# Three more late attention units in 128-byte runs: q and k in 32 or 64 loads a unit instead of 8 or 16, scores in one insertion instead of two

## The chip, the cores and the metric

The kernel runs on one core of a Trainium2 chip. The metric is the device time of one execution in microseconds (us). Engines are named as in the profile: PE (TensorE, the matmuls), PEld (its weight loads), DVE (VectorE), ACT (ScalarE), POOL (GpSimd) and SP (SyncE, which here only issues DMAs). Every engine takes its instructions in the order in which the program has them.

## The reference

Attention within chunks of 64 tokens, and two MLPs behind it, all in float32. q, k and v are (batch 8, heads 8, seq 576, head_dim 64); the 4608 tokens are 18 units of 256.

```python
def _attn_ref(q, k, v):
    ...
    scores = scale * np.matmul(q_c, k_c.transpose(0, 1, 2, 4, 3))
    scores = scores - np.max(scores, axis=-1, keepdims=True)
    attn = np.exp(scores)
    attn = attn / (np.sum(attn, axis=-1, keepdims=True) + 1e-09)
    out = np.matmul(attn, v_c)
    ...
def _moe_ref(x, w_gate, w_val, w_out, rms_g):      # 512 -> 1536 -> 512
    rms = np.sqrt(np.mean(x * x, axis=-1, keepdims=True) + 1e-06)
    xn = x / rms * rms_g
    g = xn @ w_gate
    silu = g * (1.0 / (1.0 + np.exp(-g)))
    val = xn @ w_val
    return (silu * val @ w_out).astype(np.float32)

def _moe2_ref(x, w_in, w_out):                     # 512 -> 2048 -> 512
    h = x @ w_in
    relu6 = np.clip(h + 3.0, 0.0, 6.0)
    g = h * relu6 / 6.0
    return (g @ w_out).astype(np.float32)
```

## The kernel before

The big matmuls run on pairs of numbers that are split into a high and a low part, and with sums and differences of blocks in place of some products (as in Strassen's scheme), so that most of the weights come from scratch tensors in device memory. The program goes in ticks. On a tick PE gets a group of big products, and an agenda says which other steps are put into the program at that tick. Tokens go through the first MLP in passes; in the second and third of these (366 to 765 us) the attention of later tokens is computed between the products: units 10 to 13 in the first, 14 to 17 in the second, at 0, 14, 28 and 42 ticks from its start, of 66. A pass has first the products with operands `xu` and `wo` (L1016; each `wo` load of 512 KB serves 12 of them and is issued at L463 six loads ahead of its use), then those with `gs` and `wd` (L1030, L1031, L1033; `wd` loads at L469, 512 KB).

A unit has these steps, each at a tick of its own after the unit's start (`STEPS_P`): q and k are transposed in blocks of 32 on DVE (`turn_q` at 0, `turn_k` at 1), scores on PE and their row maxima on DVE (3 and 5), the subtraction (6), exp (7), the sum and its inverse (9), the transposes of p on PE (11), the product with v (13) and squares for the RMS norm (14). Buffers for q, k, qT, kT, p and v exist once: q of the next unit can be loaded only when `turn_q` of this one is over, k when `turn_k` is.

There are two classes. `Wide`, the class of units 11, 12, 13, 15, 16 and 17, loads q and k in runs of 8 tokens of a head (2 KB in device memory), so that a 32 x 32 block transpose leaves 32 of the 64 head dimensions on a partition group; a score is the sum of two products on 32 rows, and the heads are done in two halves, `scores0`/`top0` and `scores1`/`top1`. `Pair`, the class of units 10 and 14 (and of those before 10), loads runs of 32 numbers (128 bytes), so that all 64 head dimensions stand on partitions after the transpose; one `scores` does all heads on 64 rows, one `top` all maxima. `WHOLE` names the units from 10 on that are `Pair`, and `plan_unit` then leaves out the second scores and maxima:

```python
                    if i in WHOLE and st in ("scores0", "top0"):
                        st = st[:-1]
                    elif i in WHOLE and st in ("scores1", "top1"):
                        continue
```

A unit whose 256 tokens lie in one sequence is one run of the function `runs`; where it crosses the end of a sequence of 576 it is two. Unit 13 (tokens 3328 to 3583, sequence end at 3456) is two runs of 128 tokens, units 12 and 17 are one. `Wide` issues 4 loads for each of q and k and each run (L886), `Pair` 16 (L746 or L750):

```python
                            for a in range(NP):
                                nc.sync.dma_start(out=d[r:r + 32, a, u0:u0 + un, :], in_=sv[j, g, :, a])
```

All loads go out on SP's queue. Attention loads are handed out from a list, 3 on each tick (`some(3)`), behind the wo or wd loads of that tick. `turn_k` of a unit puts the next unit's q and k into the list, `values` the next unit's v; before `turn_q` all loads of that unit which are still in the list are issued at once (`until(("qk", i))`). Every DMA of SP and of ACT takes one of eight semaphores (DMAHW0 to DMAHW7) in rotation, and an engine that issues a DMA waits until the one that had this semaphore last has landed. ACT issues the stores into scratch tensors (L286, L290: `stash_in`, `stash_out`).

Of the kernel before, what the change touches and what calls it, by code (L numbers as in the profile page):

```python
# [54 lines left out]
""".split()  # L55
SHARE_V, LOW_V = (), (2, 3)

WHOLE = (10, 14)

STEPS_P = (  # L60
    (0, ("turn_q",)),
# [30 lines left out]
def fused_kernel(  # L92
# [1004 lines left out]
    with tc.manual_schedule():  # L1097
# [24 lines left out]

        unit = [(Pair if i < 10 or i in WHOLE else Wide)(i) for i in range(NPR)]
        chain = [Half(i) for i in range(NTL, 2 * NTL)] + unit[4:]
# [37 lines left out]
        def plan_unit(i, t0):  # L1162
            for d, steps in STEPS_H if i < NTL else STEPS if t0 < P0 else STEPS_P:
                for st in steps:
# [4 lines that stand above are left out]
# [689 lines left out]
```

## Time and profile before

| | |
|---|---|
| median of 3 runs | 1649.12 us (1648.95 to 1649.36) |
| profiled execution | 1649.82 us |
| its span | 1648.0 us |
| granted TensorE clock, mean | 1.000 |
| busy: PE, DVE, ACT, POOL | 99%, 63%, 51%, 28% |
| DMA moved | 375 MB, mean 228 GB/s |

The span goes from the first to the last instruction of one profiled execution. A share is busy time over the span; engines work beside each other, so shares say which engine has time left, and only a wait on PE itself says what an edit elsewhere costs. "DMA share" in a window is the mean busy share of the 16 DMA engines.

### The profile page before, as it was taken

The page shows a single profiled execution, that of the slowest core. Times are in us where ns is not written, and L with a number is a line of the kernel's source. Part 1 is how long each engine was busy: PE and PEld are TensorE (multiplying, and loading weights), DVE is VectorE, ACT ScalarE, POOL GpSimd, SP SyncE. Part 2 cuts the span into 40 slices and gives each one's busy share as a digit, 9 for nine tenths or more (in the row PEclk, how much of TensorE's full clock was granted, in tenths as well). Part 3 has the DMA queues.
Part 4 walks back from the last instruction along what each step waited for, and adds up shares of the span by engine and source line. Part 5 has one row for each costly group of instructions (what it writes and reads, how often), then busy time and mean ns, then how long its engine had stood idle before and what let it go on. Part 6 is the DMA issues. An engine that isn't in the chain of part 4 may idle for free.

```text
span 1648.0 us, 26265 instructions
## 1 busy us (share of the span) xinstructions
PE 1636.9 (99%) x9807; PEld 1348.0 (82%) x9807; DVE 1034.8 (63%) x1532; ACT 846.0 (51%) x1410; POOL 453.4 (28%) x331
## 2 busy tenths in 40 slices
PE   8999999999999999999999999999999999999998
PEld 7888887888888888788888888888888888888887
DVE  7997566655575755638334388358746764874475
ACT  6885445455454555645434344455545544654553
POOL 1002434322236423354226522140024003301310
PEclk9999999999999999999999999999999999999999
DMA  9914777748988698855979685667877796788666
GB/s 294 287 46 108 206 211 208 209 157 243 313 277 231 203 295 269 282 216 209 331 238 334 258 283 198 219 194 244 216 216 228 213 239 200 219 230 230 191 202 156
DMA packets 352223, 375.06 MB, mean 228 GB/s; under 512 B 201440, under 2 KB 277216, under 8 KB 351968
## 3 DMA queue, kind: packets, MB, share of 16 engines
q1 hardware_dynamic: 282208, 302.32, 60.2%
q10 hardware_dynamic: 69888, 71.06, 12.7%
q8 instruction: 78, 1.28, 0.3%
q14 instruction: 49, 0.40, 0.1%
HBM read 292.55 MB, written 80.74 MB: 227 GB/s over the span
## 4 chain that ended last, share of the span: by engine, by line
PE 93%; DVE 2%; DMA 2%; SPq 2%; issue 1%; ACT 1%; POOL 0%; ACTq 0%; DVEq 0%; POOLq 0%
PE PS L1016 37%; PE PS L1595 18%; PE PS L1005 13%; PE PS L1030 6%; PE PS L1031 6%; PE PS L1033 6%; SPq L750 1%; PE PS L1042 1%; PE PS L1039 1%; PE PS L1038 1%; PE PS L837 1%; DMA q<-in_q_dram 1%; PE PS L1796 1%; PE PS L819 1%; PE PS L910 1%
## 5 line engine op out<-in xcount | busy, mean ns | idle before, releaser
L1016 PE MATMUL PS<-xu,wo 128*128 128x512 f32 x1512 | 349.8, 391 | 0.7 <-DVE s L1370 0.7
L1016 PEld LDWEIGHTS PS<-xu,wo 128*128 128x128 f32 x1512 | 282.3, 188 | 60.3 <-DVE s L1370 1.1
L1016 PE MATMUL PS<-xo,wq 128*128 128x512 f32 x1344 | 305.3, 389 | 0.0
L1595 PE MATMUL PS<-gs,wq 128*128 128x512 f32 x1296 | 295.3, 389 | 0.0
L1016 PEld LDWEIGHTS PS<-xo,wq 128*128 128x128 f32 x1344 | 252.3, 188 | 52.4
L1595 PEld LDWEIGHTS PS<-gs,wq 128*128 128x128 f32 x1296 | 242.9, 188 | 51.8 <-DVE gs L1589 1.2
L1005 PE MATMUL PS<-XH,w 128*128 128x512 f32 x576 | 146.2, 395 | 1.0 <-DVE w L222 1.0
L1005 PEld LDWEIGHTS PS<-XH,w 128*128 128x128 f32 x576 | 106.2, 188 | 24.6 <-DVE w L222 1.8
L1030 PE MATMUL PS<-gs,wd 128*128 128x512 f32 x288 | 113.2, 393 | 0.0
L1031 PE MATMUL PS<-gs,wd 128*128 128x512 f32 x288 | 112.2, 390 | 0.0
L1061 POOL TENSOR_TENSOR al<-sg,ah 128x512 fp32r<-128x512 f32 x40 | 55.9, 1396 | 155.7 <-ACT ah L1059 149.9
L1366 POOL TENSOR_TENSOR gs<-gu,gs 128x512 fp32r<-128x512 f32 x60 | 84.5, 1427 | 46.2 <-ACT gs L1365 36.3
L1370 DVE TENSOR_TENSOR gu<-gu,PS 128x512 f32<-128x512 f32 x60 | 41.1, 686 | 84.4 <-ACT gu L1452 44.1
L1663 POOL TENSOR_TENSOR gt<-gx 128x512 f32<-128x512 f32 x8 | 10.4, 1294 | 296.5 <-DVE gx L1660 296.5
L1589 DVE TENSOR_TENSOR gs<-gu,gs 128x512 fp32r<-128x512 f32 x88 | 68.0, 792 | 31.9 <-ACT gs L1588 31.6
L1588 ACT CAST gs<-gt 128x512 fp32r<-128x512 f32 x96 | 58.2, 623 | 44.1 <-DVE gt L1732 30.7
L1525 DVE SCALAR_TENSOR_TENSOR gu<-gu,PS 128x512 f32<-128x512 f32 x48 | 32.8, 684 | 72.9 <-ACT gu L1522 72.9
L1005 PE MATMUL PS<-XL,w 128*128 128x512 f32 x288 | 77.2, 390 | 0.0
L1033 PE MATMUL PS<-gs,wd 128*128 128x512 f32 x288 | 77.0, 389 | 0.0
L1059 ACT CAST ah<-sg 128x512 fp32r<-128x512 f32 x52 | 32.4, 624 | 75.5 <-DVE sg L1350 41.3
L1588 ACT CAST gs<-gu 128x512 fp32r<-128x512 f32 x96 | 57.3, 620 | 25.0 <-DVE gs L1589 17.7
L1663 POOL TENSOR_TENSOR gt<-gu 128x512 f32<-128x512 f32 x24 | 32.6, 1359 | 129.0 <-DVE gu L1660 124.8
(254 smaller groups left out, 2828.0 us busy)
## 6 DMA issues: line engine op xcount, KB each, us to landing
wq<-stash_in SPq DMA_DIRECT2D x128, 512.0 KB
wo<-ops SPq DMA_DIRECT2D x126, 512.0 KB
wq<-sums_out SPq DMA_DIRECT2D x64, 512.0 KB
wq<-stash_out SPq DMA_DIRECT2D x48, 512.0 KB
wd<-keep_out SPq DMA_DIRECT2D x36, 512.0 KB
yd<-yst SPq DMA_DIRECT2D x18, 512.0 KB
ops<-w ACTq DMA_DIRECT2D x36, 256.0 KB
v<-in_v_dram SPq DMA_DIRECT2D x32, 256.0 KB
```

Source lines behind the costliest of these rows:

```text
L1005: nc.tensor.matmul(ps, w(wi, c), xs[c][xi], start=(i == 0), stop=(i == n - 1))
L1016: nc.tensor.matmul(PS[:, bank, :], op[:, wi, c * 128:(c + 1) * 128], x[xi][:, c, :], start=first and i == 0, stop=last and i == 5, skip_gr ...
L1030: nc.tensor.matmul(ps, wm[0], a[0], start=first, stop=False)
L1031: nc.tensor.matmul(ps, wm[1], a[0], start=False, stop=False)
L1033: nc.tensor.matmul(PS[:, banks[m], :], w[:, 0, m * 128:(m + 1) * 128], a[1], start=False, stop=last)
L1061: nc.gpsimd.tensor_tensor(lo, t, hi.bitcast(F32), op=ALU.subtract)
L1366: e.tensor_tensor(w[:, 1, :], t, w[:, 0, :].bitcast(F32), op=ALU.subtract)
L1370: nc.vector.tensor_tensor(o, x, y, op=op)
L1588: nc.scalar.copy(w[:, 0, :], x)
L1589: e.tensor_tensor(w[:, 1, :], x, w[:, 0, :].bitcast(F32), op=ALU.subtract)
L1595: nc.tensor.matmul(PS[:, banks[m], :], op[:, wi, m * 128:(m + 1) * 128], x[xi], start=first and (wi, xi) == (0, 0), stop=False, skip_group ...
L1663: nc.gpsimd.tensor_tensor(slot(i, "t"), slot(i, "12"), slot(i, "11"), op=ALU.subtract)
```

## The change

`WHOLE` gains units 12, 13 and 17. They go from class `Wide` to class `Pair`.

```diff
-WHOLE = (10, 14)
+WHOLE = (10, 12, 13, 14, 17)
```

On PE, in the part with `xu` and `wo`, unit 12's scores stand like this (rows of the difference, - before, + after; L945 belongs to an RMS norm, L819 transposes unit 12's p):

```order
 L945 MATMUL PS<-sqh,ones_r 128x512
 L1016 MATMUL PS<-xu,wo 128x512 x12
-L910 MATMUL PS<-kT,qT 64x64 x32
-L1016 MATMUL PS<-xu,wo 128x512 x24
-L910 MATMUL PS<-kT,qT 64x64 x32
-L1016 MATMUL PS<-xu,wo 128x512 x72
+L781 MATMUL PS<-kT,qT 64x64 x32
+L1016 MATMUL PS<-xu,wo 128x512 x96
 L819 MATMUL PS<-ident,p 128x128 x8
```

The second insertion is gone, and the first stands where it stood. Units 13 and 17 change in the same way, among the products with `wd`.

On SP the loads of unit 13 stand, before, between the last `wo` and the first `wd` loads of the pass (numbers at scratch tensors as the program has them; v is unit 13's):

```order
L886 DMA k<-in_k_dram 16x2x512 x4
L463 DMA wo<-ops_124 128x1024 x2
L469 DMA wd<-keep_out_125 128x1024
L469 DMA wd<-keep_out_126 128x1024
...
L758 DMA v<-in_v_dram 128x8x64 x2
L469 DMA wd<-keep_out_131 128x1024
L469 DMA wd<-keep_out_132 128x1024
```

and after the change, from the first `wd` load of the pass on:

```order
L469 DMA wd<-keep_out_125 128x1024
L469 DMA wd<-keep_out_126 128x1024
L750 DMA q<-in_q_dram 32x4x32 x6
L469 DMA wd<-keep_out_127 128x1024
...
L469 DMA wd<-keep_out_130 128x1024
L750 DMA k<-in_k_dram 32x4x32 x3
L469 DMA wd<-keep_out_131 128x1024
L750 DMA k<-in_k_dram 32x4x32 x25
L758 DMA v<-in_v_dram 128x8x64 x2
L469 DMA wd<-keep_out_132 128x1024
```

The last four k loads stood two loads ahead of the first `wd`; now the last 25 stand behind the seventh. From the first q of unit 13 to its last k there are 78 loads on SP, 64 of q and k, 7 `wo` and 7 `wd`; before there were 21, 16 and 5 `wo`. In all SP issues 96 more DMAs.

With the semaphores that each waits for, the first k loads of unit 13 stand like this in the new order of SP:

```order
L469 DMA wd<-keep_out_127 128x1024 [waits DMAHW2_49,PE_49]
L469 DMA wd<-keep_out_128 128x1024 [waits DMAHW3_49]
L750 DMA q<-in_q_dram 32x4x32 [waits DMAHW5_49]
L750 DMA q<-in_q_dram 32x4x32 [waits DMAHW6_49]
L750 DMA k<-in_k_dram 32x4x32 [waits DMAHW7_49,DVE_49]
L750 DMA k<-in_k_dram 32x4x32 [waits DMAHW0_49]
```

and on ACT, whose DMAs take part in the same rotation, at that place:

```order
L1361 ACTIVATE gu<-PS 128x512 [waits PE_49]
L1452 COPY gu<-PS 128x512 [waits PE_49]
L286 DMA stash_in_113<-sc 128x2x256 [waits DMAHW4_49,Activation_49]
L286 DMA stash_in_113<-slo 128x2x256 [waits DMAHW7_49,Pool_49]
L1361 ACTIVATE gu<-gu 128x512 [waits DVE_49]
```

The DMAHW7 that the first k waits for was last taken by the second of these two stores; 34 more loads follow on SP up to unit 13's last k.

## Rows read from the trace of the kernel before

**Rows 1.** the page: busy time and share of each engine; the chain that ended last.
```profile
PE 1636.9 (99%) x9807; PEld 1348.0 (82%) x9807; DVE 1034.8 (63%) x1532; ACT 846.0 (51%) x1410; POOL 453.4 (28%) x331
...
PE 93%; DVE 2%; DMA 2%; SPq 2%; issue 1%; ACT 1%; POOL 0%; ACTq 0%; DVEq 0%; POOLq 0%
```

**Rows 2.** timeline of PE around unit 12's scores: start, length, engine, line, operation, tiles, count.
```profile
420.29 5.73 PE L1016 MATMUL PS<-xu,wo 128*128 128x512 f32 x24
425.95 1.16 PE L910 MATMUL PS<-kT,qT 32*64 32x64 f32 x64
427.04 16.62 PE L1016 MATMUL PS<-xu,wo 128*128 128x512 f32 x72
443.49 0.71 PE L819 MATMUL PS<-ident,p 128*128 128x128 f32 x5
```

**Rows 3.** timeline of PE at unit 14's scores.
```profile
576.28 1.16 PE L781 MATMUL PS<-kT,qT 64*64 64x64 f32 x64
577.37 5.97 PE L1016 MATMUL PS<-xu,wo 128*128 128x512 f32 x25
```

**Rows 4.** timeline of DVE: the q turns of units 12, 14 and 17.
```profile
458.22 2.27 DVE L890 STREAM_TRANSPOSE qT<-q 128x1024 f32<-128x1024 f32 x1
...
569.64 1.24 DVE L762 STREAM_TRANSPOSE qT<-q 128x1024 f32<-128x1024 f32 x1
...
699.14 2.16 DVE L890 STREAM_TRANSPOSE qT<-q 128x1024 f32<-128x1024 f32 x1
```

**Rows 5.** windows: stretch, its length, PE, PEld, DVE, ACT, POOL busy, PEclk, DMA share, GB/s.
```profile
124.00:139.00 15.00, 14.80 (x93) 11.64 (x92) 11.09 (x21) 8.84 (x14) 0.00 (x0) 1.00 0.21 33
...
485.00:500.00 15.00, 15.00 (x130) 12.37 (x129) 9.42 (x14) 10.12 (x17) 8.52 (x7) 1.00 1.01 363
...
501.90:524.00 22.10, 22.10 (x215) 18.03 (x214) 10.65 (x15) 9.45 (x15) 12.77 (x10) 1.00 0.95 255
...
525.00:530.00 5.00, 5.00 (x24) 4.09 (x23) 1.23 (x2) 0.56 (x2) 3.31 (x3) 1.00 0.01 0
```

**Rows 6.** timeline of SP's queue: loads of units 12, 13 and 17.
```profile
415.71 1.28 SPq L886 DMA_DIRECT2D q<-in_q_dram  x3
...
460.51 1.28 SPq L886 DMA_DIRECT2D q<-in_q_dram  x3
...
477.07 1.83 SPq L886 DMA_DIRECT2D k<-in_k_dram  x4
...
494.66 1.29 SPq L758 DMA_DIRECT2D v<-in_v_dram  x2
...
659.39 1.33 SPq L886 DMA_DIRECT2D q<-in_q_dram  x3
```

**Rows 7.** timeline of PE at unit 13's first scores.
```profile
505.63 1.16 PE L910 MATMUL PS<-kT,qT 32*64 32x64 f32 x64
```

**Rows 8.** timeline of SP's queue: loads of unit 4 (first two) and unit 14.
```profile
110.53 12.43 SPq L750 DMA_DIRECT2D q<-in_q_dram  x24
123.06 16.32 SPq L750 DMA_DIRECT2D k<-in_k_dram  x32
...
501.94 1.42 SPq L750 DMA_DIRECT2D q<-in_q_dram  x3
...
514.59 9.35 SPq L750 DMA_DIRECT2D k<-in_k_dram  x14
```

**Rows 9.** waits of SP's queue, 459 to 497: who waited <- for what: sum, times, longest.
```profile
SPq L463 <- DMA stash_in<-slo: 4.7, 1, 4.7
...
SPq L758 <- DMA stash_in<-slo: 0.5, 1, 0.5
```

**Rows 10.** timeline of ACT's DMA issues: two stores of a stash.
```profile
470.95 0.56 ACTq L286 DMA_DIRECT2D stash_in<-slo  x1
...
484.99 0.43 ACTq L286 DMA_DIRECT2D stash_in<-slo  x1
```

**Rows 11.** issues by line: L750: count, ns min/median/max, first and last start.
```profile
L750 SPq DMA_DIRECT2D q<-in_q_dram x144: 311/448/1505, 90.9 to 513.9; - x144
```

## Prediction

> **What bounds the kernel now.** I read the busy table first. TensorE works for 99% of the span and the next engine, VectorE, for 63%; the chain of waits says the same, 93% of its length is PE [rows 1]. Two things follow. Work that PE no longer does comes off the time at its full length, and a wait that PE has to take goes on top at its full length, since PE has no slack anywhere later in which to make it up. VectorE, ScalarE and the DMA queues matter here only where PE stands waiting for them. So I then read the PE timeline at the places where the late units put their scores among the big products, and the timelines of VectorE and of SP's queue around them, to see by how much each unit's q and k come ahead of their use.
>
> **What the change takes off PE.** Before, a Wide unit puts its scores into the row of big products twice, 32 instructions each time, of which the trace holds two records each (x64). In unit 12 both insertions are to be seen [rows 2]: 24 big products between them take 420.29 to 425.95, and the insertion itself holds PE from 425.95 to 427.04, 1.09 us. What it costs is a little more, for the products beside it lose some overlap. The stretch from 427.04 to 443.49 holds 72 products, 0.2285 us each; 24 of them would be 5.48 us, and from 420.29 to the end of the second insertion at 427.04 there are 6.75 us. One insertion so costs 6.75 - 5.48 = 1.27 us. The one that stays (L781, whole heads on 64 rows) holds PE from 576.28 to 577.37 in unit 14, 1.09 us as well [rows 3]: twice the rows cost no more, and the second insertion goes without anything in its place. Three units, one insertion less in each: 3 x 1.27 = 3.8; with a little for the wider gaps that I see beside the other insertions I take **-3.9 us**.
>
> **What it takes off VectorE** is worth nothing. Both turns of a unit fall from 2.2 us (L890) to 1.24 us (L762) each [rows 4], and two maxima become one. VectorE is 63% busy and PE waits for none of this, with one exception, below.
>
> **What it adds to SP's queue.** A unit's q and k come in 32 DMAs instead of 8, and unit 13, which lies across the end of a sequence, takes 64 of 16 KB instead of 16 of 64 KB. That is 24 + 48 + 24 = 96 more issues, all on SP, which issues in order, between the weight loads (wo, wd) for the products. Packets also shrink: with 128-byte runs alone the queue moved 33 GB/s at a share of 0.21, 157 GB/s at a full share; with long runs 363 at 1.01, 359 GB/s [rows 5]. A unit's q and k are 1.05 MB, so they take 6.7 us of all the DMA engines against 2.9, about 4 more per unit.
>
> Units 12 and 17 have room. Unit 12's loads began at 415.71 and its q is turned at 458.22; 43 issues stand there in the new order (32 and 11 wo), and at 0.65 us each (below) they end at 443.7. Unit 17's begin at 659.39 and end at 687.4 by the same price, while its q is turned at about 699 [rows 4, 6]. The wo and wd among them go out later by some us. They are loaded six ahead, and six times 12 products of 0.2285 us are 16 us, more than the 24 further issues cost (24 x 0.65 = 15.6), if hardly. I cost both units at nothing; if that cover is not whole, 0 to 2 us each.
>
> Unit 13 has no room. Its q cannot be loaded before unit 12's q has been turned out of the single buffer: 458.22, with the shorter turn over at 459.5 [rows 4]. Before, its 16 loads and the 5 wo among them went out from 460.51 to 478.90, and what followed was two wo, then wd and v [rows 6]. In the new order 78 issues stand from the first q to the last k, 64 small ones, 7 wo and 7 wd, and the last 25 are k alone. When is the last k there? PE reaches unit 13's scores at 505.63 before [rows 7], 1.3 earlier once unit 12 has saved its insertion: 504.3. The k turn of 1.24 us has to come first, so k must have landed by 503.1. (The order puts turn_q before it, which has its data by then.)
>
> The price of an issue is what decides. The trace has the same form of load in two settings. In unit 14, among wd loads and at a DMA share of 0.95 [rows 5], 34 issues go from 501.94 to 523.94, 0.65 us each; in unit 4, the very shape of unit 13's (64 of 16 KB, few other DMAs, share 0.21), 56 issues go from 110.53 to 139.38, 0.515 us each [rows 8]. The difference is waiting: a DMA may go only when the one 8 back in a common rotation of SP's and ACT's has landed. Unit 13's loads fall into the stretch where the share is 1.01 at its end [rows 5], and stand behind wo and wd of 512 KB, so it is nearer to unit 14. I take 0.65: 459.5 + 78 x 0.65 = 510.2. The last one lands some 2.5 us after that (an estimate: the last k of unit 14 in that stretch is issued at 523.5 and the share from 525 on is 0.01 [rows 5, 8]): 512.7. That is 512.7 - 503.1 = **9.6 us too late**.
>
> A second working, from one wait, says the same. In the new order the first k of unit 13 waits for the rotation's DMAHW7, which the second of ACT's stores of a stash holds; ACT issued it at 484.99, as its compute gets there, which follows PE. A store of this kind took about 5.7 us at the place before (issued 470.95; SP's wo waited 4.7 us for it, until just before 477.07), and this very one about 10.6 (SP's second v waited 0.5 us for it and went out at 495.57) [rows 6, 9, 10]. Now 128-byte DMAs stand ahead of it in place of wd, so I take 5.7, and its issue 1.3 earlier with all of PE's work: 483.7 + 5.7 = 489.4. The 35 issues from there at 0.65 end at 512.1, at 0.515 at 507.4; with the landing 514.6 and 509.9, so 11.5 or 6.8 us late. I stay with 9.6, between them.
>
> The bounds: if the store lands in 2.5 us (486.2) and each issue takes 0.475 (the median L750 row of 0.45 with its gap [rows 11]), the last k lands at 486.2 + 16.6 + 2.5 = 505.3, 2.2 us late. If nothing waits for the store at all and unit 4's pace holds, it lands at 459.5 + 78 x 0.515 + 2.5 = 502.2, in time. Upwards, the store takes 10.6 us (494.3) and each issue 0.65: 519.5, 16.4 us late.
>
> What is late next: PE stands at L781 with all the wd products of the down phase behind it in order, so it waits and nothing overtakes it. VectorE stands at turn_k, with the clean-up of the weight halves behind it; they are made well ahead. Unit 14's q waits for turn_q of unit 13 and its loads stand behind the late k; they move by some us, and unit 14's scores are only at 576.28, 70 us on [rows 3]. So the stall is paid once.
>
> **The sum.** 1648.0 (span) - 3.9 + 9.6 = 1653.7; the profiled execution took 1649.82 in all, so 1655.5; it lies 0.7 above the median of the runs, 1649.12, and against that median I predict **1654.8 us**.
>
> **Rivals.**
> *In time (faster).* SP's pace is the one of unit 4. Then the loads are there at 502.2 and only the gain is left: 1645.2. For it: an issue itself takes 0.45 [rows 11]; the deciding point is (503.1 - 2.5 - 459.5) / 78 = 0.53 us per issue, just above unit 4's 0.515. Against it: the DMA engines have no idle time there, the share is 1.01 from 485 on, and the wait for ACT's store is not in that pace. 0.15.
> *Half late (no change that can be told).* A stall of 0.6 to 7.2 us eats the gain. The mean of the second working at 0.515 (6.8) and of its lower bound (2.2) is 4.5, so 1649.12 - 3.9 + 4.5 = 1649.7. For it: the 25 last k issues stand together with no wd among them, and unit 4's pace is theirs. 0.27.
> *Late in full,* a stall of 7.2 to 16.4 us: my forecast, 1652.4 to 1661.6. 0.55.
> *A load costs by its count.* If a DMA of 16 KB took as long as one of 64 KB did, the 64 loads would take four times the 18.4 us that the 16 took (460.51 to 478.90 [rows 6]), 73.6 us: 533.1, with 2.5 and 1.24 a stall of 32.5 us, 1677.7. Against it: unit 4's 16 KB go at 0.515. 0.03. This would be the rule of the Trainium skill, "DMA: Bandwidth & Descriptors", "Rules for kernel authors": "Many small transfers | Coalesce into one large transfer; under 64 KB you're paying mostly overhead". The trace agrees that the packets are dearer, not that the price goes by the count alone.
>
> A difference of under 0.2%, 3.3 us, is about what these measurements cannot tell from none. So: slower 0.55 + 0.03 = 0.58 (a stall over 7.2), no difference 0.27, faster 0.15. **Range**: from 1646.0, within the case of no stall, to 1661.5, near the upper bound of the stall; it leaves out about 0.1 at either end. The likeliest case alone is 1652.4 to 1661.5.
>
> **What would show it.** In the new profile PE should stand idle once for 5 to 16 us just ahead of unit 13's L781, near 504, and the releaser should be VectorE's kT (L762), whose own wait is a DMA of k; SP's last L750 k of unit 13 should be issued at about 510. L910 should count 384 of these records and L781 704. If this wait is not there, or under 2 us, the main step is wrong and the time should be near 1645. The gain is wrong if the products from unit 12's scores to its transposes (L819) do not move up by about 1.3 us. Idle PE ahead of L1016 near 445 or of L1030 and L1031 near 690, released by a load of wo or wd, would show that units 12 and 17 had no cover either.

## The result and the profile after

The changed kernel takes 1663.48 us (median of 5 runs, 1662.18 to 1664.68) against 1649.36 us for the kernel before beside it: a ratio of 1.0082, interval 1.0070 to 1.0093, so slower by 13.5 us, 11.5 to 15.3 (the two medians are 14.1 us apart). The forecast was slower by 5.7 us, and its range ended 1.98 us below the measured time.

The profiled execution has a span of 1660.7 us, 12.7 more than before. From its page, the busy table, the granted clock over 40 slices and the chain by engine, which answer to [rows 1]:

```profile
PE 1635.3 (98%) x9615; PEld 1347.7 (81%) x9615; DVE 1028.6 (62%) x1529; ACT 846.0 (51%) x1410; POOL 453.0 (27%) x331
...
PEclk9999999999997999999999999999999999999999
...
PE 90%; DMA 5%; DVE 3%; SPq 1%; issue 1%; ACT 1%; POOL 0%; ACTq 0%; DVEq 0%; POOLq 0%
```

PE is busy for about as long as before, 1635.3 against 1636.9 us, and yet the span is 12.7 longer: PE stood still. The clock row has a 7 in its thirteenth slice (498 to 540 us); before, every slice had a 9. The view of PE's waits from 360 to 800 us says where (engine, line, waited for: sum, times, longest):

```profile
PE PS L781 <- DVE kT L762: 13.4, 1, 13.4
PE PS L1016 <- DMA wo<-ops: 0.8, 1, 0.8
```

One wait makes 13.4 us, ahead of unit 13's scores. The timeline of PE there (the bracket is idle time before, and what ended it):

```profile
503.84 1.07 PE L1033 MATMUL PS<-gs,wd 128*128 128x512 f32 x4
518.35 1.99 PE L781 MATMUL PS<-kT,qT 64*64 64x64 f32 x64 [13.44 <-DVE kT L762]
...
520.85 0.63 PE L1031 MATMUL PS<-gs,wd 128*128 128x512 f32 x1
521.28 0.63 PE L1030 MATMUL PS<-gs,wd 128*128 128x512 f32 x1
...
524.97 0.39 PE L1030 MATMUL PS<-gs,wd 128*128 128x512 f32 x1
525.19 0.40 PE L1031 MATMUL PS<-gs,wd 128*128 128x512 f32 x1
```

The 13.44 us end at 518.35, where k has been turned. Behind it stands something that the prediction did not have: the products start every 0.43 us up to 523.84, and every 0.23 us from 524.97 on. The windows over the wait, over this stretch and over the next one (columns as in [rows 5]) show the granted clock:

```profile
504.90:518.30 13.40, 0.01 (x1) 0.00 (x0) 1.25 (x2) 1.69 (x3) 2.49 (x2) 0.59 0.47 110
...
518.40:524.90 6.50, 6.50 (x76) 5.43 (x77) 4.42 (x5) 2.33 (x4) 2.28 (x2) 0.55 0.91 267
...
524.90:560.00 35.10, 35.10 (x218) 28.98 (x218) 14.68 (x18) 18.19 (x27) 21.57 (x16) 1.00 0.76 217
```

Such a figure is a mean over the window of two levels, 0.50 of full speed (1.2 GHz) and 1.00 (2.4 GHz). Narrower windows have 1.00 from 504.9 to 507.1, 0.50 from 507.3 to 518.3 and again from 518.4 to 524.2, and 1.00 from 524.4 on. So the clock fell while PE stood idle, and PE then worked at the lower level for nearly 6 us.

DVE's timeline shows the two turns of unit 13, 1.23 and 1.25 us, where [rows 4] had 1.24 for unit 14:

```profile
501.83 1.23 DVE L762 STREAM_TRANSPOSE qT<-q 128x1024 f32<-128x1024 f32 x1
517.05 1.25 DVE L762 STREAM_TRANSPOSE kT<-k 128x1024 f32<-128x1024 f32 x1 [13.98 <-DMA v<-in_v_dram]
```

q was turned at 501.83, and then DVE waited 14 us. The bracket names a load of v, which was issued just behind the last k and has a semaphore that a load of k had before it; what the k turn waits for in the program is the loads of k. SP's timeline, answering to [rows 6]:

```profile
460.24 1.32 SPq L750 DMA_DIRECT2D q<-in_q_dram  x3
...
481.72 1.59 SPq L469 DMA_DIRECT2D wd<-keep_out  x2
...
491.53 2.02 SPq L750 DMA_DIRECT2D k<-in_k_dram  x4
...
499.48 0.42 SPq L469 DMA_DIRECT2D wd<-keep_out  x1
499.95 13.51 SPq L750 DMA_DIRECT2D k<-in_k_dram  x25
```

The first q goes at 460.24, the first k at 491.53, the seventh wd at 499.48 and the last k in the row of 25 that ends at 513.46. 78 issues take 53.2 us, 0.68 each. The first 53, up to the seventh wd, take 39.7 us, 0.75 each; the 25 at the end 0.54, most of them at SP's own 0.475. SP's waits from 459 to 516 us (longest first) say what filled the first part:

```profile
SPq L750 <- DMA wo<-ops: 4.3, 3, 1.9
SPq L750 <- DMA wd<-keep_out: 3.9, 4, 2.4
SPq L463 <- DMA wo<-ops: 2.9, 3, 1.1
SPq L469 <- DMA wd<-keep_out: 2.0, 1, 2.0
```

With one more of 0.8 us, 13.9 of the 16.1 us that SP waited there ended when a wo or wd load had landed. The DMA engines themselves were not full: their share is 0.85 from 460 to 500 and 0.46 from 500 to 513.

On ACT a load of a raw weight (sraw) stands at the same place in the rotation:

```profile
512.85 0.35 ACTq L243 DMA_DIRECT2D sraw<-in_moe_w_out_dram  x1
513.24 0.62 ACT L1365 CAST gs<-gu 128x512 fp32r<-128x512 f32 x1 [12.43 <-DMA k<-in_k_dram]
```

It went out at 512.85, when the load of k that had its semaphore had landed; all of ACT's work behind it had waited 12.43 us. This load of 512 KB was then just ahead of the last k. The semaphores tell when each had landed: the k issued at 512.55, ahead of ACT's load, at 514.19, 1.6 us after its issue; ACT's load at 516.49; the last k, issued at 513.03, at 516.67, 3.6 us after its issue.

The parts that the views give add up to the 12.7 us of span. From the scores of a unit to its transposes (L819) there are 24.30 us with two insertions in unit 17 before:

```profile
705.54 1.16 PE L910 MATMUL PS<-kT,qT 32*64 32x64 f32 x64
...
729.84 1.03 PE L819 MATMUL PS<-ident,p 128*128 128x128 f32 x8
```

and 22.99 with one after:

```profile
719.57 1.16 PE L781 MATMUL PS<-kT,qT 64*64 64x64 f32 x64
...
742.56 1.03 PE L819 MATMUL PS<-ident,p 128*128 128x128 f32 x8
```

That is -1.31 for units 17 and 13 each. In unit 12 it is less. Before, 462.68 to 486.99:

```profile
462.68 1.16 PE L910 MATMUL PS<-kT,qT 32*64 32x64 f32 x64
...
469.45 1.16 PE L910 MATMUL PS<-kT,qT 32*64 32x64 f32 x64
470.54 16.62 PE L1016 MATMUL PS<-xu,wo 128*128 128x512 f32 x72
```

after, to 486.22:

```profile
462.84 1.16 PE L781 MATMUL PS<-kT,qT 64*64 64x64 f32 x64
463.93 22.44 PE L1016 MATMUL PS<-xu,wo 128*128 128x512 f32 x96
486.22 1.03 PE L819 MATMUL PS<-ident,p 128*128 128x128 f32 x8
```

so 24.31 to 23.38, -0.93; the rest went into small gaps in the row of 96, one of them a wait of 0.08 for DVE. Summed: +0.16 up to unit 12 (so far PE's program is the same), -0.93, +13.44, -1.31 and +2.68 of low clock in unit 13 (518.35 to its transposes at 544.02 are 25.67, where 22.99 are needed), -1.31 in unit 17, and -0.05 for all else: 12.7. In this last term the wait of 0.8 for a wo, ahead of 615.38, is made up by a wait of 0.7 that only the kernel before has, ahead of 678.58.

### The profile page after: what moved, and what is told of

Its sections match the earlier page's. It is cut to its first block, busy times and chain, and to the rows that moved or that the text cites. A ratio compares the mean times of both kernels' runs of the same rounds, so it can differ in the third digit from the quotient of the medians.

```text
span 1660.7 us, 25975 instructions
## 1 busy us (share of the span) xinstructions
PE 1635.3 (98%) x9615; PEld 1347.7 (81%) x9615; DVE 1028.6 (62%) x1529; ACT 846.0 (51%) x1410; POOL 453.0 (27%) x331
## 3 DMA queue, kind: packets, MB, share of 16 engines
q8 instruction: 76, 1.25, 0.3%
## 4 chain that ended last, share of the span: by engine, by line
PE 90%; DMA 5%; DVE 3%; SPq 1%; issue 1%; ACT 1%; POOL 0%; ACTq 0%; DVEq 0%; POOLq 0%
PE PS L1016 35%; PE PS L1595 18%; PE PS L1005 15%; PE PS L1030 5%; PE PS L1031 5%; PE PS L1033 5%; DMA wo<-ops 1%; DMA v<-in_v_dram 1%; PE PS L1042 1%; PE PS L1039 1%; PE PS L1038 1%; PE PS L837 1%; DMA q<-in_q_dram 1%; PE PS L1796 1%; PE PS L781 1%
## 5 line engine op out<-in xcount | busy, mean ns | idle before, releaser
L1059 ACT CAST ah<-sg 128x512 fp32r<-128x512 f32 x52 | 32.5, 624 | 74.2 <-DVE sg L1350 46.6
```

## The experiments

Theory L: all of the loss is unit 13's late k, with the low clock that follows the wait. Its rivals: S, the further loads make weights or any unit with many loads late; C, it takes units 12 and 13 together. For what makes k late: P, each issue costs SP's queue a fixed time; R, the eight DMAs in flight of SP and ACT, each of which holds its semaphore until it has landed, set the pace while loads of 512 KB are among them (eight DMAs are a lap of the rotation); D, the 128-byte packets cost the DMA engines too much; T, wd loads and ACT's stores alone, whatever the count of k's loads. Each cut of code shows the edit to the changed kernel; each ratio is to the kernel before, run beside it.

**Without unit 13.**

```diff
-WHOLE = (10, 12, 13, 14, 17)
+WHOLE = (10, 12, 14, 17)
```

> WHOLE = (10, 12, 14, 17): the change without unit 13. Theory L (all of the loss is unit 13's late k: the wait of 13.4 us and the products at the lower clock behind it): two insertions less and no wait, so 1649.4 - 2 x 1.27 = 1646.8, ratio 0.9985; no wait at L781 or L910 over 1 us. Rival S (the 24 further loads of units 12 and 17 make wo and wd late and cost what they gain): 1649 to 1651, with waits of PE on a DMA of wo or wd of 2 us or more together.

Measured: 1648.03 us against 1649.85, ratio 0.9990, interval 0.9981 to 0.9998; span 1644.7, the longest wait of PE between 360 and 800 us 0.3 us. L holds, S falls for units 12 and 17.

**All late units but 13.**

```diff
-WHOLE = (10, 12, 13, 14, 17)
+WHOLE = (10, 11, 12, 14, 15, 16, 17)
```

> WHOLE = (10, 11, 12, 14, 15, 16, 17): every late unit but 13 in 128-byte runs. Unit 11 then has 61 issues between its first q and its last k (48 of q and k, 13 wo, no wd); at the 0.63 us that an issue took in unit 13's stretch they would end at 370.5 + 38.4 = 408.9, before the turn at 417. Theory L with this price: five insertions less, 1649.4 - 5 x 1.27 = 1643.0, ratio 0.9961, no wait. Rival S (any unit with some 60 loads between weight loads is late, or makes weights late): a wait of PE of 3 us or more in unit 11 or 15 and 1648 or more.

Measured: 1655.78 us, ratio 1.0041, interval 1.0027 to 1.0055. L with its fixed price was wrong here, S was right for the two other units that cross the end of a sequence. PE's waits, 360 to 800 us:

```profile
PE PS L781 <- DVE kT L762: 7.2, 2, 4.4
PE PS L1016 <- DVE ge L1370: 1.3, 1, 1.3
```

4.45 us of the 7.2 stand ahead of unit 11's scores, 2.78 ahead of unit 15's. SP's timeline has the first q and the last k of unit 11:

```profile
370.26 1.39 SPq L746 DMA_DIRECT2D q<-in_q_dram  x3
...
409.86 10.60 SPq L750 DMA_DIRECT2D k<-in_k_dram  x9
```

370.26 to 420.46, 50.2 us for 61 issues: 0.82 each, not 0.63. There is no wd among them, but more loads of 512 KB to each small one: 13 to 48, where unit 13 has 14 to 64. SP waited 9.5 us there for wo loads, and 10.1 us for ACT's stores and raw weights, which share the rotation. The price of an issue is no constant.

**Unit 13 alone.**

```diff
-WHOLE = (10, 12, 13, 14, 17)
+WHOLE = (10, 13, 14)
```

> WHOLE = (10, 13, 14): unit 13 alone. Theory L: one insertion less, the whole wait and the low clock behind it: 1649.4 - 1.3 + 13.4 + 2.7 = 1664.2, with the wait at L781 between 12 and 15 us. Rival C (the loads of unit 12 push those of 13; together they are late): a wait under 8 us and 1658 or less.

Measured: 1660.78 us, ratio 1.0068, interval 1.0055 to 1.0081.

```profile
PE PS L781 <- DVE kT L762: 10.2, 1, 10.2
```

The wait is 10.2, under the 12 to 15 that L expected and above C's 8. From the first q to the end of the last k's issue the same 78 issues took 50.2 us (461.70 to 511.93) where the changed kernel needed 53.2: that is 3.0 of the 3.2 us. The products behind the wait lost 1.6 us at the lower clock, not 2.7. L holds in the main; whether unit 12's own loads made unit 13's issues slower in the changed kernel, as C has it in part, stays open.

**Unit 13's k in eight large loads.** In the changed kernel, for unit 13's k only (`Wide.loads` is the loop over the loads in `Wide`, made a function of its own, which the cut leaves out):

```diff
             for dst, src in ((self.q, q), (self.k, k)):
+                if self.i == 13 and src is k:
+                    yield from Wide.loads(self, dst, src)
+                    continue
```

> The changed kernel, but unit 13's k comes in Wide's 8 loads of 64 KB in place of 32 of 16 KB (k is then laid out wrongly for its scores, so unit 13's part of the result is another). Theory L: the last k is then the load in the place of SP's row 500, which went out at 499.95 and landed at 504.5 in the changed kernel, so a wait of 0 to 2 us, no fall of the clock, and all three insertions less: 1645.5 to 1647.5. Rival T (the wait comes of the other things in the rotation, the wd loads and ACT's stores, not of the count of k's loads): a wait of 8 us or more, 1655 or more.

Measured: 1652.24 us, ratio 1.0015, interval 1.0005 to 1.0025. (Lines stand 3 lower here.)

```profile
PE PS L784 <- DVE kT L765: 4.4, 1, 4.4
```

Neither expectation: 4.4 us of wait remain (in a profiled execution of 1654.44 us, 2.2 above the median). 24 loads fewer take two thirds of the wait away, so T falls as the whole cause. But the last k is late even as the 54th load from the first q: it went out at 505.82, 1.3 us behind the seventh wd, and k was turned 5.7 us later, at 511.52. The row of 25 was the larger part, not all.

**Half of unit 13's loads on ACT's queue.**

```diff
                                 for a in range(NP):
-                                    nc.sync.dma_start(out=d[r:r + 32, a, u0:u0 + un, :], in_=sv[j, g, :, a])
+                                    e = nc.scalar if self.i == 13 and a % 2 else nc.sync
+                                    e.dma_start(out=d[r:r + 32, a, u0:u0 + un, :], in_=sv[j, g, :, a])
```

> The changed kernel, but every second load of unit 13's q and k goes out on ACT's queue (32 of 64). SP then has 46 issues from the first q to the last k in place of 78; the eight semaphores are still shared by both queues. Theory P (each issue costs SP some 0.63 us, whatever stands in the rotation): 32 issues less, 20 us, so no wait and 1645.5. Theory R (the eight in flight set the pace while 512-KB loads are among them; only the last 25 k go at SP's own 0.475): the seventh wd goes out as late as before (499.5), the rest in half the time, 6 us less: a wait of about 7 us at L781, the low clock behind it, 1656 to 1658. Under R the waits for the rotation also stand in ACT's way, which can add some us.

Measured: 1655.37 us, ratio 1.0030, interval 1.0016 to 1.0043. ACT's timeline has the first load of unit 13's q and its last loads of k:

```profile
458.60 0.34 ACTq L751 DMA_DIRECT2D q<-in_q_dram  x1
...
506.68 5.16 ACTq L751 DMA_DIRECT2D k<-in_k_dram  x11
```

The last k goes out some 0.45 us before 511.84, 52.8 us after the first q; in the changed kernel the same 78 loads went from 460.24 to 513.03, 52.8 us too. With 32 issues less on SP not one microsecond was gained, and SP's own 46 still took 51.2 us (459.48 to 510.65): P falls. R had expected 6 us less for the row at the end. It did take 9.0 us on two queues instead of 13.5 on one, but the seventh wd went out at 502.82, not at 499.5, and the gain was used up. No wait for k is left at the scores, but only because PE is late by then; the waits stand elsewhere (PE, 460 to 620 us; this execution took 1659.89 us, 4.5 above the median and the longest of nine, so the median lost less than these waits):

```profile
PE PS L1031 <- ACT gs L1366: 6.2, 1, 6.2
PE PS L1017 <- ACT gu L1362: 2.9, 1, 2.9
PE PS L1017 <- DMA wo<-ops: 1.9, 1, 1.9
```

and ACT's own waits of 460 to 516 us say why:

```profile
ACT gs L1366 <- DMA k<-in_k_dram: 8.0, 1, 8.0
ACT gu L1362 <- PE PS L1017: 5.7, 1, 5.7
ACT L1362 <- DMA wo<-ops: 3.6, 1, 3.6
```

**The same 64 loads in long packets.** Each load of unit 13 brings 32 runs of 512 bytes in place of 128 of 128:

```diff
+                                    if self.i == 13:
+                                        h = 2 * a + j
+                                        nc.sync.dma_start(
+                                            out=dst.rearrange("p (a x) -> p a x", a=NP)[r:r + 32, a, u0 * 32:u0 * 32 + 128],
+                                            in_=src[b, h, s + g * 64:s + g * 64 + 64, :].rearrange("(t u) d -> t (u d)", u=2),
+                                        )
+                                        yield
+                                        continue
```

> The changed kernel, but each of unit 13's 64 loads brings 32 runs of 512 bytes instead of 128 of 128 bytes: same loads, same bytes, a quarter of the packets (what is loaded lies in another order, so unit 13's part of the result is another). Theory D (the short packets' own time on the DMA engines, 4 us more a unit, is a good part of the delay): the wait falls by 3 us or more, to under 10.5. Theories P and R: it stays at 13.4 within 1.5 us.

Measured, one run: 1661.01 us. (Lines stand 8 lower.)

```profile
PE PS L789 <- DVE kT L770: 14.0, 1, 14.0
```

14.0 us in this one execution: with a quarter of the packets the wait is no shorter. D falls.

**Six loads a tick.** Only for the ticks in which unit 13's loads are handed out:

```diff
-            some(8 if t < 0 else 5 if t < P0 - 14 else 3)
+            some(8 if t < 0 else 5 if t < P0 - 14 else 6 if P0 + 28 < t <= P0 + 42 else 3)
```

> The changed kernel, but 6 attention loads are handed out per tick instead of 3 between the k turn of unit 12 and the q turn of unit 13. From the first q to the last k of unit 13 there are then 75 issues on SP with 4 wd among them, in place of 78 with 7. Theory P: three issues less, the wait at L781 falls by 1.9 us, to about 11.5. Theory R: three 512-KB loads less ahead of the last k, and no row of 25 left at the end: the wait falls to 5 to 9 us. Under both the wd loads stand later in the queue, the first at row 56 instead of 32 of this stretch, some 10 us later; where PE then waits on a DMA of wd, the wait has only moved.

Measured: 1659.50 us, ratio 1.0055, interval 1.0038 to 1.0071. The wait for k fell further than either theory had it, to 0.9 us, and most of the time stayed lost. PE's waits, 460 to 620 us:

```profile
PE PS L1030 <- ACT gs L1365: 4.6, 2, 2.9
PE PS L1016 <- ACT s L1457: 3.4, 1, 3.4
PE PS L1016 <- DVE gu L1370: 1.9, 1, 1.9
PE PS L1016 <- ACT qT L825: 1.1, 1, 1.1
PE PS L781 <- DVE kT L762: 0.9, 1, 0.9
```

They add to 11.9 us, six waits in place of one. Part of the fall is only that PE is late by now: it came to these scores at 516.7, where the changed kernel came at 504.9. The loads themselves, from the first q to the end of the last k's issue, took 45.5 us (461.02 to 506.54) instead of 53.2, 7.7 less. With PE at its place in the changed kernel some 7 us of wait would be left (an estimate: 13.4 - 7.7, and 1.6 for the last k, which landed 5.3 us after its issue and not 3.6), within R's 5 to 9 and well under P's 11.5. The wait did move, though not to wd, as I expected, but to work of ACT, whose stores and loads stand in the same rotation behind a lap of small loads. ACT's waits, 460 to 518 us:

```profile
ACT gu L1361 <- DMA k<-in_k_dram: 8.3, 1, 8.3
...
ACT gs L1365 <- DMA k<-in_k_dram: 5.0, 1, 5.0
```

**All late units within one sequence.**

```diff
-WHOLE = (10, 12, 13, 14, 17)
+WHOLE = (10, 12, 14, 16, 17)
```

> WHOLE = (10, 12, 14, 16, 17): all late units that lie in one sequence, and none that crosses the end of one. Theory L: three insertions less and no wait over 1 us: 1649.4 - 3.8 = 1645.6, ratio 0.9977. Rival S (unit 17's 32 loads, that now follow 32 of unit 16 and stand among wd loads, come late): a wait of 2 us or more at L781 near 700, and the low clock behind it: 1650 or more.

Measured: 1647.24 us against 1649.80, ratio 0.9985, interval 0.9977 to 0.9994; span 1643.8. The longest wait of PE between 360 and 800 us:

```profile
PE PS L1016 <- ACT s L1457: 0.4, 1, 0.4
```

This is faster than the kernel before by 2.5 us, interval 1.0 to 3.8, where three insertions at 1.27 gave 3.8. L holds.

## Why the prediction was wrong in its size

**The way it goes, and where.** Right: the kernel became slower by one wait of PE, ahead of unit 13's L781, released by the turn of k, whose k came late. The records count 704 for L781 and 384 for L910. The run without unit 13 has no such wait and is faster than before.

**The gain.** Sized rightly: 3.9 forecast, 3 x 1.27 and a little, 1.31 + 1.31 + 0.93 = 3.55 measured. A place was named wrongly: the rows that I called unit 12's in [rows 2] are unit 11's, which stays Wide; unit 12's stand at 462.68 and 469.45 (above) and are of the same form, so the price was that of the right thing. Unit 12 itself gave 0.3 less than its price, in small gaps.

**The wait.** This is the step that failed: the term of 9.6 us measured 13.44. Its parts, from the working. The first q went at 460.24, not 459.5: +0.7. The issues from there to the start of the last took 52.8 us where 78 x 0.65 were 50.7: +2.1. The k turn began 4.0 after the last issue (513.03 to 517.05), where 2.5 was taken for the landing: ACT's sraw load had come ahead of it (the last k landed 3.6 us after its issue, its neighbour 1.6), +1.5. PE came 0.6 later to its place, at 504.9, as the gain of unit 12 was 0.9 and this stretch had begun 0.2 later. 9.6 + 0.7 + 2.1 + 1.5 - 0.6 = 13.3, and 13.4 unrounded with the 0.06 by which turn and scores took more. The second working, from ACT's store, came to 11.5 at the same price: the first k went at 491.53, not 489.4, and the 35 issues took 0.63 each. The store itself was priced well, issued at 484.24 and landed at 490.20; after that SP still had the last q loads in front of the first k.

**What the sum lacked.** The lower clock behind the wait, 2.68 us: a term that the working put at nothing, without a reason. It priced a stall at its own length. 13.44 lies within the bounds of the term, up to 16.4, and the total still lies outside the range, since no bound held a price for what follows an idle PE: without the 2.68 us the profiled 1662.5 would be 1659.8, within the range.

**The price of an issue.** 0.65 was close to 0.68, for a reason that was only half right and in part by luck, since 0.68 is a mean of 0.75 and 0.54. I had read it as a price per issue with waits in it; the runs show a rotation. Moving half of the issues to another engine left the time from first to last at 52.8 us, and the same kind of load went at 0.82 each in unit 11. Each DMA holds one of eight semaphores until it has landed, so eight of them take about as long as one needs to land, and that is long when 512-KB loads stand ahead of it. That this is the cause is shown as far as P and D are excluded, by SP's own waits, 13.9 of 16.1 us of them for wo and wd, and by the waits that moved to ACT when k was put ahead of wd. It holds for the first 53 loads; the 25 at the end go mostly at SP's own price of an issue. Full DMA engines, which the prediction had as a reason against the faster pace, are not it: their share was 1.01 from 485 on before, and after the change 0.85 from 460 to 500 and 0.46 from 500 to 513. That the landing time of the wo and wd loads alone sets the lap was not tried by itself: no run took them out of the rotation.

**The rival by count** (a load costs the same whatever its size) fell: it gave 32.5 us of wait. The "Rules for kernel authors" of the Trainium skill's "DMA: Bandwidth & Descriptors" pointed the right way all the same: fewer, larger loads were the faster here, 4.4 us of wait with 8 loads of k, 13.4 with 32. The packets' length, for which I had counted 4 us a unit, had no part in it.

**The rest.** Units 12 and 17 and the wo and wd among the further loads cost nothing that I can see but one wait of 0.75 us for a wo; where unit 13 stays Wide it is not there. But their loads were priced too low as well. Unit 12's 43 issues ran from 415.91 to 450.68, 0.81 each, and ended 7.0 us later than the 443.7 of the working; unit 17's ran from 674.44 to 707.15, 0.76 each, and its q was turned at 713.19, so that 6.0 us of room were left where the working had nearly 12 (its 687.4, rightly added 687.3, against 699). That these units had room was right, with less to spare than was said.

## What to carry to other kernels

A wait of the bounding engine is to be priced with what follows it: here 13.4 us of idle PE cost 2.7 more at the lower clock, and waits from 2.8 to 14.0 us in the other runs, where the clock fell, 1.4 to 2.2 more. Where two queues share a rotation of semaphores, count the DMAs of both and ask how long each holds its place; more small loads among large ones are paid in laps of the rotation, and moving them to the other queue or ahead in the order here only moved the wait. Convert only the units that have room: three units with 32 loads each gave 2.5 us, while those with 48 or 64 lost more than the insertion gave.

## What was not expected of the hardware

PE's clock fell to the lower level after waits much shorter than 13 us. From a Pair unit's scores to its transposes there are 22.99 us at the upper level. In the run with all units but 13 there were 25.12 after the wait of 4.45 us in unit 11 (0.26 of it another wait) and 24.53 after 2.78 in unit 15, and in the run with large k loads 24.34 after 4.4: 1.4 to 1.9 us on top of each. The granted clock was 0.50 behind each of these waits, from 423.2 to 426.3, 627.8 to 631.1 and 512.9 to 515.8 us. The price does not follow the length of the wait: 10.2 us in the run with unit 13 alone cost 1.6 more, 13.4 in the changed kernel 2.7 and 14.0 with long packets 2.2. A wait of 2.9 us in the run with half the loads on ACT was followed by a fall too (0.50 from 468.8 to 472.0); two waits of 2.9 and 3.4 us in the run with six loads a tick were not (1.00 from 460 to 620). What sets the difference stays open.
